# Window attention and a SoLU block on one core: the high and low parts of the probabilities multiplied apart and added in PSUM

## The chip, the core and the metric

One core of one Trainium2 chip runs the whole program. The metric is the device time of one execution in microseconds (us); less is better. Before the change the median of three runs is 497.99 us (497.97 to 498.84). A difference below about 0.2% can't be told from none.

TensorE (PE) multiplies and transposes and writes to PSUM; its weight loads are listed apart as PEld. VectorE is DVE, ScalarE is ACT, GpSimd is POOL, and SP issues the DMA transfers. Each engine works through its own queue in order.

## What is computed

The input has 4 sequences of 768 tokens with 8 heads of 64. Attention sees a window of 128 tokens back and a few sink tokens at the start of the sequence; a SoLU block with a normalisation follows, with 3072 tokens in all.

```python
scores = scale * np.matmul(q, k.transpose(0, 1, 3, 2))
keep = is_sink | in_window            # 4 sinks, window of 128
scores = np.where(keep, scores, -1000000000.0)
a = np.exp(scores - np.max(scores, axis=-1, keepdims=True))
a = a / (np.sum(a, axis=-1, keepdims=True) + 1e-09)
attn = np.matmul(a, v)
x = attn.transpose(0, 2, 1, 3).reshape(B * S, H * D)
h = x @ w_in                          # 512 -> 1024
sm = softmax(h)
solu = h * sm
ln = (solu - mu) / np.sqrt(var + 1e-06) * g_ln
return ln @ w_out                     # 1024 -> 512
```

All of it is float32.

## The kernel before

**Two parts for each number.** PE multiplies operands that are rounded to a shorter format (float32r) at a higher rate than full float32. To keep the accuracy the kernel splits an operand into a high part, the rounded value, and a low part, the remainder, and adds the products of the parts. `w1h` and `w1l`, `w2h` and `w2l` are the two parts of the weights; `xh` and `xl`, `uh` and `ul` those of the tokens.

**Chunks.** The 3072 tokens are worked on in 24 chunks of 128, numbered n. A chunk belongs to sequence b and has place c in it; two sequences alternate. Chunks with c = 0 (n = 0, 1, 12, 13) open a sequence and see neither an earlier chunk nor sinks; the first two of them (`native(n)`) are calculated in full float32. The other 22 chunks are the ones whose value products are touched by the change.

**From scores to tokens.** For each chunk: `score` multiplies queries and keys of one head into the PSUM tile `s` (264 columns, or 128 where c = 0); `mask` and `exps` make exponentials `sc`; `normalise` divides; `turn_p` transposes four heads at a time on PE. A half block hb is four heads. `p_hi` and `p_lo` write the high and the low part of the transposed probabilities into one tile `pt`, [128 keys, 4 heads, 2 parts, 128 queries]. For c > 0 `part_new` makes `pc` (what belongs to this chunk's own keys) and `part_old` leaves in `pt` what belongs to the chunk before in the sequence (n − 2).

**The value products.** The tile `vs` holds for each pair of heads the columns (head 0 high, head 0 low, head 1 low, head 1 high), 64 each. With two of these as weights, one product gives in rows 0 to 63 of PSUM the product with one part of v and in rows 64 to 127 that with the other. `value(n, pr)` works on one pair of heads, four times in a chunk: per head one product with `pc` and one with `pt`, each of 256 columns (both parts of the probabilities side by side), and one of 256 columns for the sinks of both heads, with weights `vsink` and the tile `skt`. They land in a PSUM tile `av`, [128, 2 heads, 2 parts, 128 queries].

**Adding up.** Four things have to be added for each head: two parts of v by two parts of the probabilities. `gather` adds the two parts of the probabilities with a reduction on DVE from PSUM into `y`. `shift` moves the other rows' half of `y` with two DMA transfers into `ysh`, so that both parts of v lie in the same rows, and `tokens` adds them on GpSimd into `xt`, two additions for a half block. Then `x_hi` (ScalarE) and `x_lo` (GpSimd) split `xt` into `xh` and `xl`, and `hidden` multiplies these by the first weights into `h`.

**After that** come the SoLU block with its exponential, centring and transposes (`turn_u`, tile `utp`), `u_hi`, `u_lo`, the second product `project` into `o`, `scale` and `store`.

**Buffers.** PSUM tiles `av`, `o`, `skp` (the transposed sink probabilities) and `xp` share a pool of two buffers (`ps_acc`). SBUF tiles `y`, `ysh` and `xt` have two buffers each.

**The order.** It is written out as numbers. `PLAN` gives each step a time relative to its chunk (16 units apart), `FIRST` shifts the chunks that open a sequence, `OWN` has own numbers for the first four chunks and the last two, and `PLAN_W` places the preparation of the weights. The steps are sorted by these numbers and issued in that order; each engine's queue follows from it.

Of the kernel before, what the change touches and what calls it, by code (L numbers as in the profile page):

```python
# [9 lines left out]
F32 = mybir.dt.float32  # L10
# [9 lines left out]
    "load_k": (-44.81,),  # L20
    "load_q": (-59.03,),
    "load_v": (-41.29,),
    "turn_q": (-42.19,),
    "turn_k": (-38.38,),
    "take_q": (-40.61, -40.67),
    "rest_q": (-38.96, -39.06),
    "swap_q": (-38.11, -38.3),
    "keep_k": (14.29,),
    "take_k": (-36.14, -35.45),
    "rest_k": (-35.7, -35.33),  # L30
    "ring_sinks": (-36.19,),
    "score": (-33.44, -29.74, -32.95, -26.95, -28.22, -30.8, -25.49, -21.19),
    "pick": (-32.47, -28.68, -32.31, -26.85, -27.27, -29.01, -24.23, -20.88),
    "mask": (-32.28, -28.41, -32.14, -26.44, -27.23, -28.94, -24.21, -20.59),
    "exps": (-26.81, -24.4, -23.54, -18.95),
    "invert": (-22.96, -18.09),
    "normalise": (-18.87, -15.91),
    "turn_p": (-17.35, -13.82),
    "p_hi": (-16.64, -11.13),
    "p_lo": (-15.83, -9.87),  # L40
    "part_new": (-12.34, -8.49),
    "part_old": (-10.63, -5.19),
    "sinks_hi": (-16.77, -15.48),
    "sinks_lo": (-15.95, -14.62),
    "v_hi": (-29.55, -32.12),
    "v_lo": (-13.37, -18.76),
    "sink_values": (8.06,),
    "turn_sinks": (-10.59,),
    "take_sinks": (-9.42,),
# [4 lines left out]
    "x_hi": (2.13, 8.46),  # L54
    "x_lo": (7.3, 10.78),
    "hidden": (9.12, 11.84, 11.95, 15.93, 9.13, 11.85, 13.94, 15.92),
    "highest": (18.08, 18.07),
    "peak": (18.67,),
    "solu_exp": (20.25,),
    "solu": (21.78,),  # L60
    "centre": (23.78,),
    "square": (29.22,),
    "variance": (30.73,),
    "root": (37.78,),
    "turn_u": (26.36, 26.47, 33.28, 34.25),
    "u_hi": (28.38, 35.48),
    "u_lo": (29.27, 35.93),
    "project": (32.84, 34.47, 35.03, 36.66, 37.58, 37.8, 39.25, 40.19),
    "scale": (41.34,),
    "store": (56.2,),  # L70
}
PLAN_W = {
    "round_ident": (-3163.34,),
    "gains": (-344.53, -1257.3, -494.63, -210.32, 7.7, -70.04, -35.97, -251.92, -3187.03),
    "outside": (181.94,),
    "fetch_small": (-3957.07, -334.9, -3898.57),
    "scalars": (-1567.28,),
    "spread": (-1567.18, -1257.7),
    "take_small": (-1567.08, -1257.5),
    "masks": (-1279.21, -432.35, -165.0),  # L80
    "fetch_w": (-405.15, -3960.38, -426.29, -3880.5, -3919.36, -3952.13, -3953.56, -417.09, -3892.48, -3917.91,
                -3984.79, -352.47, -151.19, -383.05, -132.13, -412.11),
    "lower_w": (-322.59, -1511.91, -340.85, -464.5, -1518.94, -3256.59, -3271.05, -342.81, -551.25, -1488.73,
                -3298.13, -259.68, -126.59, -247.18, -65.79, -329.82),
    "move_w": (-278.19, -1291.02, -319.05, -426.7, -1268.02, -2053.29, -2135.99, -342.63, -474.7, -1311.88, -2065.14,
               -242.49, -126.04, -206.92, -64.64, -318.86),
    "sign_w": (-159.49, -1266.75, -280.91, -419.12, -514.59, -2051.66, -2009.32, -327.68, -447.58, -1267.77,
               -2054.73, -219.39, -79.66, -139.64, -54.37, -316.39),
    "rest_w": (-155.59, -517.15, -155.98, -388.61, -341.51, -2042.38, -1259.65, -242.66, -366.45, -1238.15, -521.74,
               -206.56, -69.38, -91.58, -32.25, -243.78),  # L90
    "sum_w": (-119.83, -422.04, -96.33, -336.21, -229.53, -1475.65, -702.46, -156.13, -302.03, -648.8, -436.66,
              -80.12, 29.82, -32.53, 15.53, -217.15),
    "w_hi": (-128.31, -479.01, -100.46, -341.71, -328.13, -1468.88, -984.48, -230.1, -337.05, -577.13, -482.82,
             -120.05, -19.66, -38.33, -27.91, -142.74),
    "less_w": (-118.42, -381.66, -88.15, -328.34, -206.16, -1389.51, -691.27, -137.84, -264.23, -448.45, -338.06,
               -54.35, 33.19, -26.02, 16.19, -99.77),
    "w_lo": (-100.5, -348.23, -79.88, -324.36, -159.61, -1257.51, -570.51, -129.19, -260.8, -350.76, -260.82, -44.19,
             33.91, -21.12, 20.58, -87.29),
# [3 lines left out]
    "load_k": -44.94, "load_q": -26.01, "load_v": -1.72, "turn_q": -0.63, "turn_k": -1.52, "take_q": -0.56,  # L102
    "rest_q": 1.16, "swap_q": 1.2, "keep_k": -15.24, "take_k": -2.22, "rest_k": -0.04, "ring_sinks": 19.87,
    "score": -0.52, "pick": -141.4, "mask": 0.1, "exps": -0.49, "invert": 0.8, "normalise": 1.65, "turn_p": 2.88,
    "p_hi": 2.39, "p_lo": 3.57, "part_new": -91.77, "part_old": 14.12, "sinks_hi": -15.13, "sinks_lo": 80.96,
    "v_hi": 6.27, "v_lo": 0.87, "sink_values": -17.46, "turn_sinks": -111.76, "take_sinks": 33.57, "value": -0.23,
    "gather": -0.6, "shift": -0.41, "tokens": 1.81, "x_hi": 0.92, "x_lo": 0.06, "hidden": -0.59, "highest": -1.19,
    "peak": -0.51, "solu_exp": 2.24, "solu": 1.9, "centre": 0.58, "square": -3.38, "variance": -3.55, "root": 0.7,
    "turn_u": 0.05, "u_hi": 1.02, "u_lo": 0.95, "project": 0.45, "scale": 4.92, "store": -8.36,
}  # L110
OWN = {
# [61 lines left out]
P = 128  # L173
# [56 lines left out]
def _banded(ctx, tc, q, k, v, n_sink, window, w_in, w_out, g_ln, out, val, wts, wpool, consts):  # L230
# [467 lines left out]
    def take_sinks(n, _):  # L698
        if place(n)[1] > 0:
            tr = st["skp", n]  # L700
            skt = st["skt", n] = sb.tile([P, 2, P], F32R, tag="skt", name=f"skt_{n}", bufs=2)
            for i, m in enumerate((even, odd)):
                nc.scalar.activation(skt[:, i, :], tr.bitcast(F32), AF.Copy, scale=m)

    def value(n, pr):
        b, c = place(n)
        hb, jp = divmod(pr, HB // 2)
        alone = c == 0
# [333 lines left out]
```

## Time and profile before

| | |
|---|---|
| median of three runs | 497.99 us |
| the profiled execution | 498.57 us |
| its span, first to last instruction | 496.9 us |
| mean granted clock of PE | 0.988 |
| products on PE, as many weight loads | 2631 |
| transfers of `ysh` / of `qX` | 88 / 88 |

A profile page has the busy time of each engine first, then the span in 40 slices of 12.4 us in which a digit is the busy share in tenths. Lines of groups name the source line, the engine, the operation, output and inputs by the program's tile names, the shape and count, then busy us and mean ns of one, and the idle time of the engine just before them with what ended it. A product's length reaches from its start to its modelled end, and products overlap; the distance from one start to the next tells what a product takes of PE. In the view of waits a line says who waited for whom, with total us, times and the longest.

### The profile page before, as it was taken

To read this page: it belongs to the slowest core of one execution; us is meant where nothing else is said; L and a number is where in the kernel's file an instruction comes from. 1 tells how busy PE (TensorE), PEld (TensorE's weight loads), DVE (VectorE), ACT (ScalarE), POOL (GpSimd) and SP (SyncE) were. 2 spreads that over 40 slices of the span, in tenths; PEclk is the share of its full clock that TensorE was granted. 3 is DMA by queue.
4 is the path that set the end of the run, shared out by engine and by line. 5 is a ranking of instruction groups with operands and counts; after the bars stand their busy time and mean duration, and the time that the engine had idled before them with its cause. 6 is when DMAs were issued, how large, how long until landed. Compare 5 with 4: busy or idle time off the path is not lost.

```text
span 496.9 us, 9093 instructions
## 1 busy us (share of the span) xinstructions
PE 468.7 (94%) x2631; PEld 388.4 (78%) x2631; DVE 390.5 (79%) x1195; ACT 354.4 (71%) x957; POOL 316.1 (64%) x439
## 2 busy tenths in 40 slices
PE   0989999999899999999999999999999999999995
PEld 0444767888788888888888888888888888887873
DVE  2878999899987588798799988888888879766631
ACT  4798997787785667776876786676777787675352
POOL 3675576588666557678646386676776776667610
PEclk9978999999999999999999999999999999999999
DMA  8966154354265353522555363464264262201101
GB/s 275 307 196 171 43 108 106 85 122 113 61 140 119 75 117 84 120 67 54 119 136 106 79 139 68 113 138 107 53 141 106 54 144 61 57 28 44 44 22 47
DMA packets 101099, 51.78 MB, mean 104 GB/s; under 512 B 78956, under 2 KB 90228, under 8 KB 101044
## 3 DMA queue, kind: packets, MB, share of 16 engines
q1 hardware_dynamic: 101044, 51.14, 42.4%
q8 instruction: 23, 0.38, 0.3%
q14 instruction: 32, 0.26, 0.2%
HBM read 27.53 MB, written 6.42 MB: 68 GB/s over the span
## 4 chain that ended last, share of the span: by engine, by line
PE 73%; DVE 9%; ACT 5%; POOL 5%; issue 4%; DMA 2%; SPq 0%; DVEq 0%; POOLq 0%
PE o L841 22%; PE h L772 21%; PE s L606 4%; PE s L607 4%; PE utp L826 4%; PE av L721 3%; PE ptp L652 3%; PE av L724 3%; PE ws L441 2%; PE kt L526 2%; PE qt L526 2%; PE av L726 1%; DVE y L734 1%; DVE ring L579 1%; DMA wraw<-in_moe_w_in_dram 1%
## 5 line engine op out<-in xcount | busy, mean ns | idle before, releaser
L841 PE MATMUL o<-w2h,uh 128*128 128x512 f32 x192 | 79.2, 412 | 0.0
L772 PE MATMUL h<-w1h,xh 128*128 128x512 f32 x192 | 77.5, 403 | 0.6 <-DVE u L794 0.6
L634 ACT ACTIVATE sc<-sc,nmx 128x136 f32<-128x136 f32 (+1 forms) x192 | 76.4, 402 | 1.7 <-DVE nmx L624 1.2
L772 PE MATMUL h<-w1l,xh 128*128 128x512 f32 x192 | 75.9, 395 | 0.0
L841 PE MATMUL o<-w2h,ul 128*128 128x512 f32 x192 | 75.7, 394 | 0.0
L734 DVE TENSOR_REDUCE y<-av 128x256 f32<-128x512 f32 x88 | 60.3, 687 | 19.5 <-PE av L726 17.0
L772 PE MATMUL h<-w1h,xl 128*128 128x512 f32 x192 | 75.7, 394 | 0.0
L841 PE MATMUL o<-w2l,uh 128*128 128x512 f32 x192 | 75.6, 394 | 0.0
L669 POOL TENSOR_SCALAR_AFFINE_SELECT pc<-pt 128x1024 fp32r<-128x1024 f32 x40 | 43.8, 1095 | 33.3 <-DVE pt L662 17.0
L624 DVE CUSTOM_DVE_ANT_0 sc<-s,bias 128x136 f32<-128x136 f32 (+1 forms) x192 | 54.4, 295 | 10.1 <-PE s L604 2.9
L645 POOL TENSOR_TENSOR sc<-sc,rs 128x544 f32<-128x544 f32 (+1 forms) x48 | 52.2, 1089 | 15.5 <-DVE rs L640 8.7
L606 PE MATMUL s<-ring,qT 128*128 128x264 f32 (+1 forms) x176 | 56.2, 321 | 2.6 <-DVE nmx L624 1.4
L761 POOL TENSOR_TENSOR xl<-xt,xh 128x256 fp32r<-128x256 f32 x44 | 32.4, 737 | 28.9 <-ACT xh L756 22.5
L607 PE MATMUL s<-ring,qX 128*128 128x264 f32 (+1 forms) x176 | 49.7, 285 | 0.3 <-DMA qX<-qT 0.3
L721 PE MATMUL av<-pc,vs 128*128 128x256 f32 x160 | 44.3, 299 | 1.3 <-ACT ob L846 0.9
L675 POOL TENSOR_SCALAR_AFFINE_SELECT pt<-pt 128x1024 fp32r<-128x1024 f32 x40 | 43.6, 1091 | 1.6
L830 ACT CAST uh<-utp 128x512 fp32r<-128x512 f32 x48 | 28.0, 586 | 21.3 <-PE utp L826 21.1
L834 DVE TENSOR_TENSOR ul<-utp,uh 128x512 fp32r<-128x512 f32 x48 | 33.0, 687 | 12.8 <-ACT uh L830 12.1
L772 PEld LDWEIGHTS h<-w1h,xl 128*128 128x128 f32 x192 | 36.1, 188 | 8.9
L841 PEld LDWEIGHTS o<-w2h,ul 128*128 128x128 f32 x192 | 36.1, 188 | 8.7 <-DVE ul L834 0.2
L606 PEld LDWEIGHTS s<-ring,qT 128*128 128x128 f32 x176 | 33.1, 188 | 11.9 <-issue 3.6
L574 ACT CAST ring<-kt 64x512 fp32r<-64x512 f32 x44 | 25.4, 578 | 22.9 <-DVE ring L579 21.8
(147 smaller groups left out, 1300.7 us busy)
## 6 DMA issues: line engine op xcount, KB each, us to landing
qX<-qT SPq DMA_DIRECT2D x88, 128.0 KB, 2.2
kn<-in_k_dram SPq DMA_DIRECT2D x24, 256.0 KB, 3.5
qn<-in_q_dram SPq DMA_DIRECT2D x24, 256.0 KB, 4.1
vn<-in_v_dram SPq DMA_DIRECT2D x24, 256.0 KB, 4.3
out_dram<-ob SPq DMA_DIRECT2D x24, 256.0 KB, 3.5
ysh<-y SPq DMA_DIRECT2D x88, 64.0 KB, 2.0
wraw<-in_moe_w_out_dram SPq DMA_DIRECT2D x8, 512.0 KB, 4.0
wraw<-in_moe_w_in_dram SPq DMA_DIRECT2D x8, 512.0 KB, 6.6
```

Source lines behind the costliest of these rows:

```text
L606: nc.tensor.matmul(o, st["qT", n, x][:, r, :], rhs, start=True, stop=False)
L607: nc.tensor.matmul(o, st["qX", n, x][:, r, :], rhs, start=False, stop=True)
L624: nc.vector.tensor_tensor_reduce(out=st["sc", n, hb][:, j, c0:c1], in0=st["s", n, h].rearrange("p a x -> p (a x)")[:, c0:c1], in1=bias0 if ...
L634: nc.scalar.activation(sc[:, i, c0:c1], sc[:, i, c0:c1], AF.Exp, bias=nmx[:, i:i + 1], scale=-1.0, accum_out=ssum[:, i:i + 1])
L645: nc.gpsimd.tensor_tensor(sc[:, :, c0:c1], sc[:, :, c0:c1], rs.unsqueeze(2).to_broadcast([P, HB, c1 - c0]), op=ALU.mult)
L669: nc.gpsimd.affine_select(pc, pt.bitcast(F32), pattern=[[0, HB * 2], [1, P]], compare_op=ALU.is_ge, fill=0.0, base=0, channel_multiplier=-1)
L675: nc.gpsimd.affine_select(pt, pt.bitcast(F32), pattern=[[0, HB * 2], [-1, P]], compare_op=ALU.is_ge, fill=0.0, base=-1, channel_multiplier=1)
L721: nc.tensor.matmul(acc[:, x], lhs, pc[:, 2 * jp + x], start=(x == 0), stop=(alone and x == 1))
L734: nc.vector.tensor_reduce(st["y", n, hb][:, jp], st["acc", n, pr].rearrange("p x s q -> p x q s"), axis=AX.X, op=ALU.add)
L772: nc.tensor.matmul(st["h", n][:, cols], a[:, kt % 2, :], w[:, kt, cols], start=(kt == 0 and m == 0), stop=(kt == KT1 - 1 and m == 2))
L834: nc.vector.tensor_tensor(ul, st["utp", n, g4], st["uh", n, g4].bitcast(F32), op=ALU.subtract)
L841: nc.tensor.matmul(st["o", n], a[:, kt % 4, :], part(w, kt), start=(kt == 0 and m == 0), stop=(kt == KT2 - 1 and m == 2))
```

## The change

`value` now works on a half block (two pairs of heads) at a time, so that it stands twice in a chunk, not four times. Each product of 256 columns becomes two of 128, one for the high part of the probabilities (t = 0) and one for the low part (t = 1), with the same weights and into the same 128 columns of PSUM, where they are added up. The tile `av` now holds [128, 2 pairs, 2 heads, 128 queries] and serves the whole half block. The sinks' product stays at 256 columns.

`gather`, `shift` and the tile `y` are gone. A new step `lower` copies the half of `av` that lies in the other rows into `ysh` with ScalarE, and `tokens` adds the other half to it on DVE, straight from PSUM. Both have two instructions of 64 rows by 256 elements for a half block.

All numbers of `PLAN`, `FIRST`, `OWN` and `PLAN_W` are new; one line of them stands here for all.

```diff
 PLAN = {
-    "value": (-5.58, -9.27, -2.3, -0.4),
-    "gather": (-4.96, -7.67, -1.44, 1.33),
-    "shift": (-3.45, 1.72),
-    "tokens": (0.47, 7.55),
+    "value": (-8.65, 1.15),
+    "lower": (-7.68, 3.4),
+    "tokens": (-7.23, 3.74),
...
-    def value(n, pr):
+    def value(n, hb):
...
-        acc = st["acc", n, pr] = ps_acc.tile([P, 2, 2, P], F32, tag="acc", name=f"av_{n}_{pr}")
-        for x in range(2):
-            lhs = st["vs", n, hb][:, jp, 2 * x:2 * x + 2, :].rearrange("p t d -> p (t d)")
-            nc.tensor.matmul(acc[:, x], lhs, pc[:, 2 * jp + x], start=(x == 0), stop=(alone and x == 1))
+            if jp == 0:
+                acc = st["acc", n, hb] = ps_acc.tile([P, HB // 2, 2, P], F32, tag="acc", name=f"av_{n}_{hb}")
+            parts = [(n, pc)] if alone else [(n, pc), (n - 2, pt)]
+            for x in range(2):
+                for m, p_ in parts:
+                    lhs = st["vs", m, hb][:, jp, 2 * x:2 * x + 2, :].rearrange("p t d -> p (t d)")
+                    for t in range(2):
+                        nc.tensor.matmul(acc[:, jp, x, :], lhs, p_[:, 2 * jp + x, t, :],
+                                         start=(x == 0 and m == n and t == 0),
+                                         stop=(alone and x == 1 and t == 1))
             if not alone:
-                lhs = st["vs", n - 2, hb][:, jp, 2 * x:2 * x + 2, :].rearrange("p t d -> p (t d)")
-                nc.tensor.matmul(acc[:, x], lhs, pt[:, 2 * jp + x], start=False, stop=False)
-        if not alone:
-            nc.tensor.matmul(acc[:, :, 0, :], st["vsink", b][:, pr, :], st["skt", n], start=False, stop=True)
+                nc.tensor.matmul(acc[:, jp], st["vsink", b][:, pr, :], st["skt", n], start=False, stop=True)
...
-        nc.vector.tensor_reduce(st["y", n, hb][:, jp], st["acc", n, pr].rearrange("p x s q -> p x q s"),
-                                axis=AX.X, op=ALU.add)
...
-        nc.sync.dma_start(ysh[0:D], y[D:P, :, 0, :])
-        nc.sync.dma_start(ysh[D:P], y[0:D, :, 1, :])
...
-        nc.gpsimd.tensor_tensor(xt[0:D], y[0:D, :, 0, :], ysh[0:D], op=ALU.add)
-        nc.gpsimd.tensor_tensor(xt[D:P], y[D:P, :, 1, :], ysh[D:P], op=ALU.add)
+    def lower(n, hb):
...
+        for x in range(2):
+            nc.scalar.copy(ysh[ROWS[x]], st["acc", n, hb][ROWS[1 - x], :, x, :])
...
+        for x in range(2):
+            nc.vector.tensor_tensor(xt[ROWS[x]], st["acc", n, hb][ROWS[x], :, x, :], st["ysh", n, hb][ROWS[x]], op=ALU.add)
```

In the rows below the names carry chunk, half block or pair, and a running number: `av_11_1` is chunk 11's tile for pair 1 before, and `av_11_0` that for half block 0 afterwards.

PE before, at the second pair of chunk 11:

```order
L606 MATMUL s_12_6_3340<-ring_124,qT_12_0_3089 128x128
L607 MATMUL s_12_6_3340<-ring_124,qX_12_0_3158 128x128
L721 MATMUL av_11_1_3349<-pc_11_0_3289,vs_11_0_3001 128x256
L724 MATMUL av_11_1_3349<-pt_11_0_3215,vs_9_0_2447 128x256
L721 MATMUL av_11_1_3349<-pc_11_0_3289,vs_11_0_3001 128x256
L724 MATMUL av_11_1_3349<-pt_11_0_3215,vs_9_0_2447 128x256
L726 MATMUL av_11_1_3349<-skt_11_3346,vsink_1_927 128x2x128
L841 MATMUL o_8_3244<-w2h_3_521,uh_8_1_3287 128x512
```

PE now, at the same half block of chunk 11, of which the first pair and the start of the second are shown:

```order
L831 MATMUL o_8_3354<-w2h_2_608,ul_8_1_3398 128x512
L722 MATMUL av_11_0_3428<-pc_11_0_3374,vs_11_0_3067 128x128 x2
L722 MATMUL av_11_0_3428<-pt_11_0_3288,vs_9_0_2487 128x128 x2
L722 MATMUL av_11_0_3428<-pc_11_0_3374,vs_11_0_3067 128x128 x2
L722 MATMUL av_11_0_3428<-pt_11_0_3288,vs_9_0_2487 128x128 x2
L726 MATMUL av_11_0_3428<-skt_11_3400,vsink_1_1140 128x256
L722 MATMUL av_11_0_3428<-pc_11_0_3374,vs_11_0_3067 128x128 x2
```

Five products per pair became nine, and both pairs of a half block now stand in one run of eighteen, where before each pair's five stood apart between other work.

PE now, from the end of chunk 10's last value products on. Six more products into `o_8` and then `skp_11` follow; `skp_11` takes the `ps_acc` buffer that `av_10_1` has held:

```order
L726 MATMUL av_10_1_3310<-skt_10_3127,vsink_0_658 128x256
L522 MATMUL qt_13_3333<-ident_89,qn_13_2697 128x128 x4
L602 MATMUL s_12_1_3344<-ring_124,qT_12_1_3142 128x128
L603 MATMUL s_12_1_3344<-ring_124,qX_12_1_3202 128x128
L648 MATMUL ptp_11_1_3349<-ident_89,sc_11_1_3050 128x128 x4
L831 MATMUL o_8_3354<-w2h_0_245,uh_8_0_3241 128x512
L831 MATMUL o_8_3354<-w2l_0_246,uh_8_0_3241 128x512
L831 MATMUL o_8_3354<-w2h_0_245,ul_8_0_3245 128x512
L602 MATMUL s_12_4_3366<-ring_124,qT_12_0_3144 128x128
```

Eight transposes, four scores and nine products of 512 columns stand between the last value product of chunk 10 and the sinks' transpose of chunk 11.

DVE before, around the first half block of chunk 11:

```order
L734 TENSOR_REDUCE y_11_0_3384<-av_11_1_3349 128x256
L639 TENSOR_SCALAR rs_12_0_3400<-ssum_12_0_3225 128x4
L640 RECIPROCAL rs_12_0_3400<-rs_12_0_3400 128x4
L557 TENSOR_TENSOR qT_13_1_3355<-qt_13_3314,qT_13_1_3355 64x512
L557 TENSOR_TENSOR qT_13_0_3357<-qt_13_3314,qT_13_0_3357 64x512
L734 TENSOR_REDUCE y_11_0_3384<-av_11_0_3412 128x256
```

DVE now, at the same place:

```order
L553 TENSOR_TENSOR qT_13_1_3418<-qt_13_3333,qT_13_1_3418 64x512
L553 TENSOR_TENSOR qT_13_0_3420<-qt_13_3333,qT_13_0_3420 64x512
L742 TENSOR_TENSOR xt_11_0_3467<-av_11_0_3428,ysh_11_0_3460 64x256 x2
L635 TENSOR_SCALAR rs_12_0_3475<-ssum_12_0_3292 128x4
L636 RECIPROCAL rs_12_0_3475<-rs_12_0_3475 128x4
```

The two reductions are replaced by two additions in one place, which read `ysh_11_0` that ScalarE's two copies write. On ScalarE these copies stand ahead of the exponentials of chunk 12 and of `xh_11_0`.

More of the change, by code (lines that the diff above doesn't have):

```diff
@@ L64 @@
[L64 to L70, printed above, removed]
+    "load_k": (-42.11,),
+    "load_q": (-56.77,),
+    "load_v": (-40.64,),
+    "turn_q": (-42.08,),
+    "turn_k": (-38.33,),
+    "take_q": (-40.71, -40.74),
+    "rest_q": (-39.71, -39.83),
+    "swap_q": (-36.9, -38.18),
+    "keep_k": (16.66,),
+    "take_k": (-36.03, -35.95),
@@ new lines @@
+    "rest_k": (-35.93, -35.59),
+    "ring_sinks": (-37.22,),
+    "score": (-33.6, -30.15, -33.83, -27.32, -28.37, -31.53, -26.07, -20.81),
+    "pick": (-33.39, -29.96, -33.7, -26.66, -27.87, -30.58, -24.45, -20.23),
+    "mask": (-31.87, -28.4, -32.39, -26.45, -27.72, -30.49, -24.37, -20.22),
+    "exps": (-23.69, -23.17, -19.12, -19.11),
+    "invert": (-22.5, -18.36),
+    "normalise": (-21.74, -16.4),
+    "turn_p": (-17.82, -12.73),
+    "p_hi": (-16.75, -11.19),
+    "p_lo": (-16.32, -8.73),
@@ new lines @@
+    "part_new": (-11.64, -5.81),
+    "part_old": (-11.53, -5.08),
+    "sinks_hi": (-17.18, -15.11),
+    "sinks_lo": (-16.87, -13.95),
+    "v_hi": (-29.9, -31.63),
+    "v_lo": (-12.23, -20.21),
+    "sink_values": (9.27,),
+    "turn_sinks": (-11.15,),
+    "take_sinks": (-9.87,),
+    "value": (-8.65, 1.15),
+    "lower": (-7.68, 3.4),
+    "tokens": (-7.23, 3.74),
+    "x_hi": (-6.19, 4.81),
+    "x_lo": (-5.05, 8.49),
+    "hidden": (10.53, 11.7, 13.21, 14.61, 7.5, 11.71, 13.2, 16.91),
+    "highest": (17.71, 17.72),
@@ L71 @@
+    "peak": (18.98,),
+    "solu_exp": (20.8,),
+    "solu": (22.39,),
+    "centre": (23.96,),
+    "square": (31.56,),
+    "variance": (36.13,),
+    "root": (37.67,),
+    "turn_u": (26.8, 26.46, 30.84, 30.62),
+    "u_hi": (28.16, 33.03),
+    "u_lo": (28.71, 37.94),
+    "project": (35.34, 36.02, 36.56, 37.29, 38.56, 39.34, 39.39, 42.47),
+    "scale": (44.9,),
+    "store": (58.0,),
 }
 PLAN_W = {
-    "round_ident": (-3163.34,),
-    "gains": (-344.53, -1257.3, -494.63, -210.32, 7.7, -70.04, -35.97, -251.92, -3187.03),
@@ L75 @@
[L75 to L84, printed above, removed]
@@ L97 @@
-    "w_lo": (-100.5, -348.23, -79.88, -324.36, -159.61, -1257.51, -570.51, -129.19, -260.8, -350.76, -260.82, -44.19,
-             33.91, -21.12, 20.58, -87.29),
+    "round_ident": (-1322.39,),
+    "gains": (-368.15, -1165.53, -479.33, -225.74, -20.3, -46.93, -60.03, -262.5, -3645.13),
+    "outside": (211.35,),
+    "fetch_small": (-4191.48, -394.17, -4097.18),
+    "scalars": (-1537.76,),
+    "spread": (-1368.02, -1361.85),
+    "take_small": (-1358.56, -1336.69),
+    "masks": (-1097.56, -360.46, -185.65),
@@ new lines @@
+    "sign_w": (-227.21, -621.59, -467.19, -417.3, -573.87, -2082.04, -1376.57, -338.9, -576.28, -1319.96, -2083.31,
+               -210.97, -119.38, -128.9, -79.1, -366.13),
+    "rest_w": (-173.68, -604.59, -319.07, -404.26, -377.17, -1351.58, -1346.0, -317.8, -571.46, -1311.07, -1320.96,
+               -171.48, -109.56, -122.6, -69.94, -359.9),
+    "sum_w": (-128.69, -443.97, -113.39, -361.19, -269.27, -1347.16, -530.33, -174.79, -364.93, -549.25, -475.14,
+              -145.58, -13.22, -36.37, 27.53, -248.08),
@@ new lines @@
+    "w_hi": (-159.19, -519.26, -113.21, -324.89, -327.46, -1325.09, -1307.62, -283.17, -477.5, -509.0, -1268.36,
+             -148.15, -31.62, -94.11, 30.19, -173.9),
+    "less_w": (-125.3, -417.49, -109.98, -313.61, -215.74, -1292.57, -517.46, -174.67, -308.17, -400.9, -453.55,
+               -130.49, -8.51, -31.52, 30.44, -123.76),
+    "w_lo": (-122.59, -378.07, -92.59, -284.69, -189.42, -1264.65, -485.74, -151.02, -283.72, -378.99, -383.81,
+             -129.95, -4.1, -21.98, 32.36, -112.0),
@@ L107 @@
-    "gather": -0.6, "shift": -0.41, "tokens": 1.81, "x_hi": 0.92, "x_lo": 0.06, "hidden": -0.59, "highest": -1.19,
-    "peak": -0.51, "solu_exp": 2.24, "solu": 1.9, "centre": 0.58, "square": -3.38, "variance": -3.55, "root": 0.7,
-    "turn_u": 0.05, "u_hi": 1.02, "u_lo": 0.95, "project": 0.45, "scale": 4.92, "store": -8.36,
+    "load_k": -44.89, "load_q": -25.65, "load_v": 6.01, "turn_q": -4.31, "turn_k": 1.85, "take_q": -0.49,
+    "rest_q": 0.01, "swap_q": 0.6, "keep_k": -15.73, "take_k": -0.34, "rest_k": 0.19, "ring_sinks": 20.63,
@@ new lines @@
+    "score": 0.23, "pick": -141.32, "mask": -0.21, "exps": -0.17, "invert": 0.83, "normalise": 2.08, "turn_p": 1.83,
+    "p_hi": 1.7, "p_lo": 1.86, "part_new": -101.27, "part_old": 13.79, "sinks_hi": -15.91, "sinks_lo": 83.7,
+    "v_hi": -0.04, "v_lo": -0.3, "sink_values": -12.59, "turn_sinks": -108.85, "take_sinks": 34.56, "value": -1.18,
+    "lower": -0.7, "tokens": 0.05, "x_hi": 0.57, "x_lo": 1.43, "hidden": -0.13, "highest": -0.13, "peak": 1.2,
+    "solu_exp": 1.97, "solu": 0.74, "centre": 0.26, "square": 0.73, "variance": -1.65, "root": 2.29, "turn_u": -0.06,
@@ L728, in gather @@
-    def gather(n, pr):
+        pc = pt if alone else st["pc", n, hb]
+        for jp in range(HB // 2):
+            pr = hb * (HB // 2) + jp
+            if native(n):
+                if ("xp", n, hb) not in st:
+                    st["xp", n, hb] = ps_acc.tile([P, HB // 2, P], F32, tag="acc", name=f"xp_{n}_{hb}")
+                for x in range(2):
+                    nc.tensor.matmul(st["xp", n, hb][ROWS[x], jp, :], st["vn", n][:, 2 * pr + x, :],
+                                     pt[:, 2 * jp + x, 0, :], start=True, stop=True)
+                continue
+            if jp == 0:
+                acc = st["acc", n, hb] = ps_acc.tile([P, HB // 2, 2, P], F32, tag="acc", name=f"av_{n}_{hb}")
+            parts = [(n, pc)] if alone else [(n, pc), (n - 2, pt)]
+            for x in range(2):
+                for m, p_ in parts:
[4 more added lines that the diff above has]
+                                         stop=(alone and x == 1 and t == 1))
+            if not alone:
+                nc.tensor.matmul(acc[:, jp], st["vsink", b][:, pr, :], st["skt", n], start=False, stop=True)
@@ L729, in gather @@
+    def lower(n, hb):
         if native(n):
             return
-        hb, jp = divmod(pr, HB // 2)
-        if ("y", n, hb) not in st:
-            st["y", n, hb] = sb.tile([P, HB // 2, 2, P], F32, tag="y", name=f"y_{n}_{hb}", bufs=2)
-        nc.vector.tensor_reduce(st["y", n, hb][:, jp], st["acc", n, pr].rearrange("p x s q -> p x q s"),
-                                axis=AX.X, op=ALU.add)
-    def shift(n, hb):
-        if native(n):
-            return
-        y = st["y", n, hb]
         ysh = st["ysh", n, hb] = sb.tile([P, HB // 2, P], F32, tag="ysh", name=f"ysh_{n}_{hb}", bufs=2)
-        nc.sync.dma_start(ysh[0:D], y[D:P, :, 0, :])
-        nc.sync.dma_start(ysh[D:P], y[0:D, :, 1, :])
+        for x in range(2):
+            nc.scalar.copy(ysh[ROWS[x]], st["acc", n, hb][ROWS[1 - x], :, x, :])
@@ L855, in _banded @@
               score, pick, mask, exps, invert, normalise, turn_p, p_hi, p_lo, part_new, part_old, sinks_hi, sinks_lo,
-              v_hi, v_lo, sink_values, turn_sinks, take_sinks, value, gather, shift, tokens, x_hi, x_lo,
+              v_hi, v_lo, sink_values, turn_sinks, take_sinks, value, lower, tokens, x_hi, x_lo,
               hidden, highest, peak, solu_exp, solu, centre, square, variance, root, turn_u, u_hi, u_lo,
```

73 lines of the change are left out of this document (7 added, 66 removed), and 109 rows, old and new, of the table OWN.

## The prediction

> **What bounds the kernel now.** I read the busy times first, then the slices, then busy time by stretch.
>
> ```profile
> span 496.9 us, 9093 instructions
> PE 468.7 (94%) x2631; PEld 388.4 (78%) x2631; DVE 390.5 (79%) x1195; ACT 354.4 (71%) x957; POOL 316.1 (64%) x439
> PE   0989999999899999999999999999999999999995
> PEclk9978999999999999999999999999999999999999
> ```
>
> PE leads with 94% of the span, and its slices show where the other 6% lie: in the first slices and at the end. The granted clock is full but for the start, so products run at one speed from about 40 us on. The view of busy time by stretch gives the share in the middle (columns: length, then each engine's busy us and count, clock, DMA):
>
> ```profile
> 0.00:80.00 80.00, 62.21 (x283) 40.42 (x284) 61.61 (x182) 64.34 (x167) 45.08 (x81) 0.94 0.64 177
> 80.00:460.00 380.00, 375.77 (x2200) 323.14 (x2199) 314.91 (x984) 275.71 (x766) 261.00 (x346) 1.00 0.41 95
> 460.00:497.00 37.00, 30.70 (x152) 24.80 (x151) 14.00 (x30) 14.40 (x25) 10.02 (x14) 0.97 0.12 38
> ```
>
> From 80 to 460 us PE is busy 375.8 of 380 us. It is the bound there, with 4.2 us idle, while DVE has 65 us to spare, ScalarE 104 and GpSimd 119. All `av` products but a few lie in that stretch. Whatever PE gets to do there in addition lengthens the kernel by nearly its full size; whatever DVE, GpSimd or the DMA queue are spared can return 4.2 us at most there. The view of waits says what PE waited for:
>
> ```profile
> PE spread L302 <- POOL alone L296: 7.3, 1, 7.3
> PE ws L441 <- DVE wbits L424: 4.7, 1, 4.7
> PE av L721 <- ACT ob L846: 0.9, 2, 0.7
> ```
>
> The two long waits belong to the scalars and the weights at the start, which the change does not touch (only their places in the order shift). The rest are below 2 us each in sum. No wait of PE names `gather`, `shift` or `tokens` as its releaser for more than fractions of a microsecond.
>
> **What the change puts on PE.** The groups of instructions give the counts (line, names, shape, count, busy us, mean ns):
>
> ```profile
> L721 PE MATMUL av<-pc,vs 128*128 128x256 f32 x160 | 44.3, 299 | 1.3 <-ACT ob L846 0.9 <-DVE y L734 0.3
> L724 PE MATMUL av<-pt,vs 128*128 128x256 f32 x160 | 41.5, 281 | 0.0
> L721 PE MATMUL av<-pt,vs 128*128 128x256 f32 x16 | 3.5, 300 | 0.0
> ```
>
> That is 336 products of 256 columns. Each becomes two of 128 columns that add into the same 128 columns of PSUM: 672 in place of 336. The 80 sink products keep their 256 columns. The mean of about 0.28 us is one product's length from its start to its modelled end; products overlap, so the price is the distance between starts. The timeline of PE shows it for one pair of heads (start, length):
>
> ```profile
> 184.60 0.28 PE L721 MATMUL av<-pc,vs 128*128 128x256 f32 x1
> ...
> 185.07 0.28 PE L726 MATMUL av<-skt,vsink 128*128 128x256 f32 x1
> 185.19 0.40 PE L841 MATMUL o<-w2h,uh 128*128 128x512 f32 x1
> ```
>
> From 184.60 to 185.19 us stand five products (the three left out are the other two of L721 and L724 and start between): 0.59 / 5 = **0.118 us** for one of 256 columns.
>
> A product of 128 columns in the same number format stands in this trace too: the scores of the chunks that open a sequence. Four of them lie between products of 512 columns:
>
> ```profile
> 253.24 0.40 PE L841 MATMUL o<-w2h,ul 128*128 128x512 f32 x1
> 253.47 0.22 PE L606 MATMUL s<-ring,qT 128*128 128x128 f32 x1
> 253.53 0.27 PE L607 MATMUL s<-ring,qX 128*128 128x128 f32 x1
> 253.65 0.28 PE L606 MATMUL s<-ring,qT 128*128 128x128 f32 x1
> 253.76 0.27 PE L607 MATMUL s<-ring,qX 128*128 128x128 f32 x1
> 253.87 0.45 PE L841 MATMUL o<-w2h,uh 128*128 128x512 f32 x1
> 254.16 0.39 PE L841 MATMUL o<-w2l,uh 128*128 128x512 f32 x1
> ```
>
> A product of 512 columns takes 0.23 us (253.24 to 253.47). From 253.47 to 254.16 are 0.69 us for four of 128 columns and one of 512: (0.69 − 0.23) / 4 = **0.115 us** each. Half the columns cost almost the same. Why, the weight loads of the same stretch tell:
>
> ```profile
> 253.48 0.19 PEld L607 LDWEIGHTS s<-ring,qX 128*128 128x128 f32 x1
> 253.59 0.19 PEld L606 LDWEIGHTS s<-ring,qT 128*128 128x128 f32 x1
> 253.70 0.19 PEld L607 LDWEIGHTS s<-ring,qX 128*128 128x128 f32 x1
> 253.81 0.19 PEld L841 LDWEIGHTS o<-w2h,uh 128*128 128x128 f32 x1
> ```
>
> Loads follow each other at 0.11 us and no closer. A product of 256 columns just covers the next load; one of 128 doesn't, and the load sets the pace. The change reads the two 128-column parts against the same weights, so the question is whether the second load is made. Before has the same case, `uh` against `w2h` and then against `w2l`:
>
> ```profile
> L841 PEld LDWEIGHTS o<-w2l,uh 128*128 128x128 f32 x192 | 36.3, 189 | 4.2 <-issue 0.2
> L841 PEld LDWEIGHTS o<-w2h,uh 128*128 128x128 f32 x192 | 36.2, 189 | 4.5 <-PE ptp L652 0.2
> ```
>
> Each of the two has its own 192 loads: equal weights are loaded again.
>
> So PE gets 672 × 0.112 − 336 × 0.118 = 75.3 − 39.6 = **+35.6 us**, with 0.112 between the load's 0.110 and the measured 0.115. By the ends: 672 × 0.110 gives +34.3, 672 × 0.115 gives +37.6.
>
> The Trainium skill speaks against this rate in one place: TensorE: Matmul & The Clock Gate, section Back-to-back issue gap, has about 81 ns per product of 128 columns for a stream of load and product. By that the 672 would take 54.4 us and the change +14.8 us. The rows above, 0.110 to 0.115 us, don't agree; what they leave of it is the second rival.
>
> **What it takes from the others and puts on them.**
>
> ```profile
> L734 DVE TENSOR_REDUCE y<-av 128x256 f32<-128x512 f32 x88 | 60.3, 687 | 19.5 <-PE av L726 17.0 <-issue 2.0 <-POOL pc L669 0.4
> L751 POOL TENSOR_TENSOR xt<-y,ysh 64x256 f32<-64x256 f32 x44 | 32.1, 730 | 10.0 <-DMA ysh<-y 6.8 <-DVE z L802 3.1
> L752 POOL TENSOR_TENSOR xt<-y,ysh 64x256 f32<-64x256 f32 x44 | 32.3, 734 | 3.3
> ysh<-y SPq DMA_DIRECT2D x88, 64.0 KB, 2.0
> L756 ACT CAST xh<-xp 128x256 fp32r<-128x256 f32 x4 | 1.5, 364 | 0.0
> L761 DVE TENSOR_TENSOR xl<-xp,xh 128x256 fp32r<-128x256 f32 x4 | 1.7, 417 | 0.0
> ```
>
> Gone: 88 reductions (60.3 us of DVE), 88 additions on GpSimd (32.1 + 32.3 = 64.4 us), 88 transfers of `ysh` on SP's queue at 2.0 us to landing. New: 88 copies from PSUM on ScalarE and 88 additions from PSUM on DVE, each of 256 elements in 64 rows. The nearest rows with 256 elements from PSUM take 364 and 417 ns, so 32.0 and 36.7 us. These operations aren't in the trace with 64 rows; the ends I take are half these prices and the 687 ns of the reduction, at most 60.5 us on either engine. ScalarE comes to 354.4 + 32.0 = 386.4 us (415 at the upper end), DVE to 390.5 − 60.3 + 36.7 = 366.9 us (at most 390.7), GpSimd to 316.1 − 64.4 = 251.7 us. None nears PE's 468.7 + 35.6 = 504.3 us, so all of this is hidden behind PE, in both directions, and I cost it at nothing. If the cover went, ScalarE's part would be the first to show.
>
> The path from an `av` tile to `x_lo` gets shorter: two transfers and two additions of 0.73 us go, two copies and two additions, 2 × 0.364 + 2 × 0.417 = 1.56 us, come. That can return part of the 4.2 us that PE idles in the middle. Ends: nothing and 4.2; I take 3.
>
> **Sum.** The profiled execution took 498.57 us (0.6 above the median 497.99 of three, inside their spread to 498.84). 498.6 + 35.6 − 3 = 531.2, so **531 us**. This case's own range: from the median, 498.0 + 34.3 − 4.2 = 528, less 4 for a start that may come out better in the new order, 524; above, 498.6 + 37.6 with nothing returned and 6 us of new waits, 542.
>
> **Rivals.**
>
> First, the other side: **the second product pays no load.** If equal weights were kept, or their load fully hidden, a product of 128 columns would cost 0.059 us, half of 0.118; PE would get nothing, 672 × 0.059 = 39.6 for 39.6, and the shorter path would return 3 us: 498.6 − 3 = 495.6, faster. It decides below (39.6 + 3) / 672 = 0.063 us per product. For it: the recorded starts 253.47 and 253.53 lie 0.06 apart. Against: the next starts lie 0.12 and 0.11 apart, the 512-column product after the four takes 0.29 in place of 0.23, and the doubled loads of `uh`. 4 in 100. That the change doesn't do what it says, in that a repeated load is dropped, comes to the same.
>
> Second, **every other load is half hidden.** If all pairs went like the first (253.47 to 253.65, 0.18 us for two), PE would get 336 × (0.18 − 0.118) = +20.8: 498.6 + 20.8 − 3 = 516 us. Against: the first pair follows a long product, under which its loads began; in a run of 16 only the first does. 10 in 100.
>
> Third, **a new wait for PSUM.** The sinks' transpose `skp` takes the buffer that the last `av` tile of the chunk before held, which now is free only after copies and additions, 1.56 us and the waits in two queues; both queues run in order, so a late copy holds up the exponentials behind it, and the addition behind it on DVE holds up the masks. In front of `skp` stand nine products of 512 columns alone, 9 × 0.23 = 2.1 us, and more. If it came 1 us late in each of the 20 chunks with sinks, 498.6 + 35.6 + 20 = 554 us. 9 in 100.
>
> **Chances.** 77 in 100 for 524 to 542 us, 10 for the second rival, 9 for the third, 4 for the first. The range 513 to 544 holds the likeliest case and the second rival, 0.87 by these numbers; the third is left out above and the first below, and the half-hidden load keeps the low end. A difference under 0.2% (1 us) can't be told from none here. Faster 0.03, same 0.01, slower 0.96: the first rival alone can end faster or near no change.
>
> **What would show it.** PEld with 2631 + 336 = 2967 loads and `av` starts 0.11 us apart through a run of eight: right. Starts 0.06 apart: the first rival. PE 98 to 100% busy in the middle, with a total near 504 us, and DVE about 367, ScalarE 386, GpSimd 252: right. A wait of `skp` or `av` for the copies or additions above 10 us in all: the third rival. The prediction fails if a product of 128 columns costs well under 0.11 us in a long run, or if PE waits more in the new order than in the old.

## The result and the profile after

The changed kernel takes 525.14 us (median of four runs, 524.73 to 529.21), the kernel before 498.06 us beside it: a ratio of 1.055, with an interval of 1.052 to 1.058. It is slower by 27 us. The forecast was 531 us, in a range from 513 to 544.

The page after, first lines:

```profile
span 523.7 us, 9609 instructions
PE 500.8 (96%) x2967; PEld 420.6 (80%) x2967; DVE 370.1 (71%) x1195; ACT 390.1 (74%) x1045; POOL 255.0 (49%) x351
PE   1989999999999999999999999999999999999994
```

PE is busy for 32.1 us longer (500.8 against 468.7) with 336 more products and 336 more loads, and it idles for 22.9 us of the span where it idled for 28.2. PE's sum stays 3.5 us under the 504.3 of the prediction; the account below comes back to that. DVE, ScalarE and GpSimd come within 4 us of theirs. Busy time by stretch, after (columns as in the prediction):

```profile
0.00:80.00 80.00, 66.21 (x318) 43.80 (x319) 62.20 (x184) 67.36 (x176) 46.81 (x83) 0.98 0.68 187
80.00:460.00 380.00, 378.55 (x2350) 330.51 (x2349) 282.96 (x939) 291.65 (x801) 189.83 (x246) 1.00 0.32 78
460.00:487.00 27.00, 27.00 (x161) 23.22 (x161) 14.26 (x48) 16.88 (x45) 13.49 (x16) 1.00 0.05 20
487.00:524.00 37.00, 29.06 (x143) 23.11 (x141) 10.67 (x27) 14.18 (x24) 4.87 (x7) 0.97 0.07 24
```

In the middle PE now idles for 1.5 of 380 us (4.2 before), in the first 80 us for 13.8 (17.8 before), and the granted clock of that stretch is 0.98 instead of 0.94. DVE has 97 us to spare in the middle, GpSimd 190. The longest waits of PE, after:

```profile
PE spread L298 <- POOL alone L292: 9.1, 1, 9.1
PE ws L437 <- DVE wbits L420: 1.1, 1, 1.1
PE o L831 <- ACT ob L836: 0.8, 2, 0.5
```

No wait of `skp` or `av` for the new copies and additions (`ysh`, `xt`) is in that view, which goes down to 0.2 us. The products themselves, the timeline of PE after, at one half block (x2: two products in a row with one line and one pair of tiles):

```profile
206.96 0.33 PE L722 MATMUL av<-pc,vs 128*128 128x128 f32 x2
207.13 0.39 PE L722 MATMUL av<-pt,vs 128*128 128x128 f32 x2
207.35 0.39 PE L722 MATMUL av<-pc,vs 128*128 128x128 f32 x2
207.58 0.38 PE L722 MATMUL av<-pt,vs 128*128 128x128 f32 x2
207.80 0.34 PE L726 MATMUL av<-skt,vsink 128*128 128x256 f32 x1
207.98 0.33 PE L722 MATMUL av<-pc,vs 128*128 128x128 f32 x2
...
208.81 0.34 PE L726 MATMUL av<-skt,vsink 128*128 128x256 f32 x1
208.99 0.40 PE L831 MATMUL o<-w2h,uh 128*128 128x512 f32 x1
```

Behind the first pair, pairs of products stand 0.22 us apart, 0.11 each. The eighteen products of the half block take 208.99 − 206.96 = 2.03 us; the ten of before took 2 × 0.59 = 1.18. The loads of the same half block:

```profile
207.07 0.30 PEld L722 LDWEIGHTS av<-pt,vs 128*128 128x128 f32 x2
207.30 0.30 PEld L722 LDWEIGHTS av<-pc,vs 128*128 128x128 f32 x2
207.52 0.30 PEld L722 LDWEIGHTS av<-pt,vs 128*128 128x128 f32 x2
207.74 0.19 PEld L726 LDWEIGHTS av<-skt,vsink 128*128 128x128 f32 x1
```

Each pair shows two loads of the same weights, and pairs of loads too are 0.22 us apart. What replaced the reductions and the transfers:

```profile
L734 ACT COPY ysh<-av 64x256 f32<-64x256 f32 x88 | 32.3, 367 | 17.4 <-PE av L726 16.4
L742 DVE TENSOR_TENSOR xt<-av,ysh 64x256 f32<-64x256 f32 x88 | 37.1, 421 | 21.6 <-ACT ysh L734 19.6
```

367 and 421 ns, where 364 and 417 were taken. DVE waits for the copies 19.6 us in sum, and none of it shows as a wait of PE.

### The profile page after: what moved, and what is told of

Its sections match the earlier page's. It is cut to its first block, busy times and chain, and to the rows that moved or that the text cites. A ratio compares the mean times of both kernels' runs of the same rounds, so it can differ in the third digit from the quotient of the medians.

```text
span 523.7 us, 9609 instructions
## 1 busy us (share of the span) xinstructions
PE 500.8 (96%) x2967; PEld 420.6 (80%) x2967; DVE 370.1 (71%) x1195; ACT 390.1 (74%) x1045; POOL 255.0 (49%) x351
## 4 chain that ended last, share of the span: by engine, by line
PE 84%; DVE 2%; ACT 1%; issue 1%; DMA 1%; DVEq 0%; ACTq 0%
PE h L762 25%; PE o L831 23%; PE av L722 14%; PE s L602 4%; PE utp L816 4%; PE s L603 4%; PE ptp L648 3%; PE av L726 3%; PE qt L522 2%; PE kt L522 2%; DMA wraw<-in_moe_w_out_dram 1%; ACT ob L836 1%; PE ws L437 0%; DVE u L784 0%; DMA qX<-qT 0%
## 5 line engine op out<-in xcount | busy, mean ns | idle before, releaser
L831 PE MATMUL o<-w2h,uh 128*128 128x512 f32 x192 | 80.7, 420 | 1.0 <-ACT ob L836 0.8
L722 PE MATMUL av<-pt,vs 128*128 128x128 f32 x352 | 66.1, 275 | 0.0
L620 DVE CUSTOM_DVE_ANT_0 sc<-s,bias 128x136 f32<-128x136 f32 (+1 forms) x192 | 55.6, 294 | 12.9 <-PE s L603 6.7
L722 PE MATMUL av<-pc,vs 128*128 128x128 f32 x320 | 58.3, 264 | 0.0
L722 PEld LDWEIGHTS av<-pc,vs 128*128 128x128 f32 x320 | 51.1, 190 | 3.4 <-issue 0.5
L722 PEld LDWEIGHTS av<-pt,vs 128*128 128x128 f32 x352 | 52.4, 192 | 0.0
L742 DVE TENSOR_TENSOR xt<-av,ysh 64x256 f32<-64x256 f32 x88 | 37.1, 421 | 21.6 <-ACT ysh L734 19.6
L609 DVE COPY_PREDICATED s<-m_cur,s 128x128 f32<-128x128 int32 x96 | 27.5, 291 | 32.6 <-PE s L603 31.8
L734 ACT COPY ysh<-av 64x256 f32<-64x256 f32 x88 | 32.3, 367 | 17.4 <-PE av L726 16.4
```

What stands on the lines that cost most here:

```text
L620: nc.vector.tensor_tensor_reduce(out=st["sc", n, hb][:, j, c0:c1], in0=st["s", n, h].rearrange("p a x -> p (a x)")[:, c0:c1], in1=bias0 if ...
L722: nc.tensor.matmul(acc[:, jp, x, :], lhs, p_[:, 2 * jp + x, t, :], start=(x == 0 and m == n and t == 0), stop=(alone and x == 1 and t == 1))
L734: nc.scalar.copy(ysh[ROWS[x]], st["acc", n, hb][ROWS[1 - x], :, x, :])
L742: nc.vector.tensor_tensor(xt[ROWS[x]], st["acc", n, hb][ROWS[x], :, x, :], st["ysh", n, hb][ROWS[x]], op=ALU.add)
L831: nc.tensor.matmul(st["o", n], a[:, kt % 4, :], part(w, kt), start=(kt == 0 and m == 0), stop=(kt == KT2 - 1 and m == 2))
```

## The experiments

Two questions are open in the result. Is the price of the products really the 35.6 us of the prediction, when only 27 us came out? And what returned the rest? Each run's median stands beside that of the kernel before on the same chip; comparisons with the changed kernel go by its 525.14 us, which was measured apart from these runs.

### The split alone, in the old order

The kernel before, with the value products alone split; they write the same columns as before, and `gather`, `shift`, `tokens` and the order stay.

```diff
-            nc.tensor.matmul(acc[:, x], lhs, pc[:, 2 * jp + x], start=(x == 0), stop=(alone and x == 1))
+            for t in range(2):
+                nc.tensor.matmul(acc[:, x, t, :], lhs, pc[:, 2 * jp + x, t, :], start=(x == 0 and t == 0),
+                                 stop=(alone and x == 1 and t == 1))
...
```

The product with `pt` is split in the same way.

> The kernel before with nothing changed but the value products: each of 256 columns becomes two of 128, which write the same columns of av as before; gather, shift, tokens and the order stay. If a product of 128 columns costs a weight load, 0.112 us (theory), PE gets the full 35.6 us and the old order returns at most the 4.2 us of its idle time in the middle: 529 to 534 us. If the 27 us of the change are the price of the products alone (rival: 0.099 us per product, nothing returned elsewhere): 525 us. If the second product of equal weights pays no load: 498 us.

Measured: 529.61 us against 498.69, a ratio of 1.062 (1.060 to 1.065), 31 us more. Its first 80 us and its middle stretch:

```profile
0.00:80.00 80.00, 62.26 (x300) 41.10 (x301) 61.62 (x182) 64.47 (x168) 47.41 (x83) 0.98 0.66 180
80.00:460.00 380.00, 378.32 (x2349) 331.62 (x2347) 303.50 (x932) 259.33 (x722) 242.60 (x320) 1.00 0.41 92
```

That is the theory's case, and the split by itself costs more than the whole change. PE idles for 1.7 us of the middle, where it idled for 4.2: the old order returns its idle time there too, with the old path. So shorter transfers were not needed for that; PE having more to do was enough.

### The new order and path without the split

The changed kernel with value products of 256 columns.

```diff
-                    for t in range(2):
-                        nc.tensor.matmul(acc[:, jp, x, :], lhs, p_[:, 2 * jp + x, t, :],
...
+                    nc.tensor.matmul(acc[:, jp], lhs, p_[:, 2 * jp + x],
...
```

> The changed kernel with its order and its copies and additions, but the value products back at 256 columns, 336 of them, written over both heads' columns of av, so that the parts of the probabilities are not added up but mixed between heads. If the products cost 35.6 us and new order and path return some 8 us (theory): 525.1 - 35.6 = 489 to 491 us, under the kernel before. If the products cost 27 us and nothing is returned (rival): 498 us.

Measured: 492.31 us against 498.69, a ratio of 0.989 (0.984 to 0.995), with runs from 489.9 to 495.8. The median lies 1 us above the theory's range, far from the rival's 498. It is 6 us under the kernel before, and 33 us under the changed kernel; the sums are mixed between heads, so this is a measurement and no replacement. With the run above this makes a table of four, and the split costs 31 us in the one order and 33 in the other:

| | products of 256 | products of 128 |
|---|---|---|
| old order and path | 498.7 | 529.6 |
| new order and path | 492.3 | 525.1 |

### Fewer columns, as many products

The changed kernel, the low part's products with 32 columns.

```diff
                     for t in range(2):
-                        nc.tensor.matmul(acc[:, jp, x, :], lhs, p_[:, 2 * jp + x, t, :],
+                        w = P if t == 0 else 32
+                        nc.tensor.matmul(acc[:, jp, x, 0:w], lhs, p_[:, 2 * jp + x, t, 0:w],
```

> The changed kernel with the low part's products of 32 columns in place of 128: three quarters of the low part of the probabilities are left out, the number of products stays. If the load sets the pace (theory), no change: 524 to 526 us. If the columns did (rival), 336 x 0.04 = 13 us less: 512 us.

Measured: 523.79 us (522.88 to 524.25), 1.3 us below the changed kernel. Of the 13 us that the columns would have given, nothing is to be seen beyond that. PE's timeline at a half block:

```profile
206.20 0.29 PE L723 MATMUL av<-pc,vs 128*128 128x128 f32 x2
206.34 0.37 PE L723 MATMUL av<-pt,vs 128*128 128x128 f32 x2
206.56 0.38 PE L723 MATMUL av<-pc,vs 128*128 128x128 f32 x2
...
208.02 0.36 PE L727 MATMUL av<-skt,vsink 128*128 128x256 f32 x1
208.22 0.40 PE L832 MATMUL o<-w2h,uh 128*128 128x512 f32 x1
```

Here x2 stands for one product of 128 and one of 32 columns. The half block takes 208.22 − 206.20 = 2.02 us, against 2.03 with full columns. The columns don't set the pace; what stays the same is one load of 128 columns for each product.

### Half the products

The changed kernel without the low part's products.

```diff
-                    for t in range(2):
+                    for t in range(1):
...
```

> The changed kernel without the low part's products: 336 products of 128 columns in place of 672. Theory: 336 x 0.112 = 37.6 us less, 487 to 489 us, hardly below 336 products of 256 columns. Rival (0.099 us per product): 492 us. If the second product of equal weights pays no load, 336 x 0.06 = 20 us less: 505 us.

Measured: 488.66 us against 498.69, a ratio of 0.981 (0.979 to 0.983): 36.5 us below the changed kernel, 0.109 us for each of the 336 products taken out. It leaves out the low part of the probabilities and is no replacement. It is only 3.6 us under the run with 336 products of 256 columns: the second 128 columns of such a product are nearly free.

### Where the rest was returned: the order at the start

Four runs put the new numbers under the old steps. The first takes the preparation of the weights and chunks 0 to 3 from the new order, with products of 256 columns and `gather`, `shift` and `tokens`.

```diff
 PLAN_W = {
-    "round_ident": (-3163.34,),
+    "round_ident": (-1322.39,),
...
-    "scalars": (-1567.28,),
+    "scalars": (-1537.76,),
```

> The kernel before with its own steps and 256-column products; only the order of the weights' preparation and of the first four chunks follows the changed kernel's numbers (its value steps split into two pairs, with gather, shift and tokens spaced out behind them). If the part that was returned at the start comes from the order there (theory): 4 to 7 us less than before, 491 to 494 us. If it comes from the shorter path through copies and additions, or from fewer DMA transfers (rival): 498 us, or more where the two orders join badly.

Measured: 510.88 us against 498.43, a ratio of 1.026 (1.023 to 1.029): slower by 12 us. The theory's total (491 to 494) is missed, and what came is the rival's open end, "or more where the two orders join badly", so the total can't tell where the start's gain comes from. The first product into `h` shows the start apart from it; the timelines of PE before, after and in this run:

```profile
54.92 0.47 PE L772 MATMUL h<-w1h,xh 128*128 128x512 f32 x1
```

```profile
50.52 0.39 PE L762 MATMUL h<-w1h,xh 128*128 128x512 f32 x1
```

```profile
49.75 0.39 PE L704 MATMUL h<-w1h,xh 128*128 128x512 f32 x1
```

The lead of 4 to 5 us is there with the old steps, 20 us before the first value product (70 us): it can't come from the new path. A part of it is the clock's: the split in the old order, whose clock at the start was that of the changed kernel (0.98 in the first 80 us), has this product at 53.0 us. The lead is lost later, first in the stretch where the two orders meet:

```profile
80.00:130.00 50.00, 43.83 (x252) 35.76 (x251) 42.37 (x131) 32.83 (x98) 33.95 (x44) 1.00 0.40 87
```

PE idles for 6.2 of 50 us there (0.9 before), and for 9.0 us between 130 and 460 us, where it was 3.4 before.

The second puts all of the new order under the old steps.

> The kernel before with its own steps and 256-column products, and all of its order after the changed kernel's numbers, the value steps split as in the other run. Theory: the order at the start returns 4 to 7 us, the middle is bound by PE as before: 489 to 494 us. Rival (the path returned it, the order does nothing): 498 us. If reductions and transfers don't fit the other order, new waits: above 500 us.

Measured: 543.35 us against 498.43, a ratio of 1.090 (1.087 to 1.093): the third case of the expectation, new waits. The largest of them is that of the scores for the moved queries:

```profile
PE s L539 <- DMA qX<-qT: 15.3, 17, 2.4
```

Their transfers share SP's queue with those of `ysh`, and these hold the queue up more than before while they wait for the reductions:

```profile
SPq L674 <- DVE y L666: 205.9, 37, 14.9
```

The same wait was 117.8 us before. PE idles for 58.3 us of this span, 30 us more than before; the rest of the 45 us isn't accounted for.

Two more runs were to join the start better, with the new numbers for the weights and chunks 0 and 1 alone, and for chunks 0 to 3 but for the steps from `value` to the split of x.

> The kernel before with its own steps and 256-column products; the order of the weights' preparation and of the first two chunks alone follows the changed kernel's numbers, chunks 2 and 3 keep their old places. If the start is returned by the order (theory) and the old order of chunks 2 and 3 joins it well: first hidden product at 49 to 51 us instead of 53 to 55, and 493 to 496 us in all, faster than before. If the order of the start returns nothing that lasts (rival): 498 us or more, because PE waits later by as much.

> As the run with two chunks, but chunks 2 and 3 too follow the changed kernel's numbers up to the value products and from the hidden products on; value, gather, shift, tokens and the split of x keep their old places where the inputs are there in time. Theory: as above, 493 to 496 us. Rival: 498 us or more.

Measured: 506.04 us against 498.76, ratio 1.016 (1.012 to 1.019), and 512.09 us against the same, ratio 1.028 (1.024 to 1.032). Their first products into `h` start at 51.7 and 49.5 us, and neither keeps the lead: both totals are the rival's. A better start under the old order gave no faster kernel here.

### The new path in the old order

The changed kernel's steps with the old numbers: `value` at the place of the second pair, copies and additions right behind.

```diff
-    "value": (-8.65, 1.15),
-    "lower": (-7.68, 3.4),
-    "tokens": (-7.23, 3.74),
+    "value": (-5.58, -0.4),
+    "lower": (-5.08, 0.1),
+    "tokens": (-4.78, 0.4),
```

> The changed kernel's steps (products of 128 columns, copies on ScalarE, additions on DVE) in the old order: value at the place of the second pair, copies and additions right behind it, all else where the kernel before has it. If the shorter path returns only idle time of the middle and the new order returns the rest at the start (theory): as the split products in the old order, 527 to 530 us. If the path returned all of it (rival): 524 to 526 us, as the changed kernel.

> The same old order and new steps with value products of 256 columns over both heads' columns (the parts of the probabilities are mixed between heads, not added up): the path alone against the kernel before. Theory: the idle time of the middle at most, 494 to 498 us. Rival (the path returned all): 490 to 492 us. If the copies and additions wait badly in the old order: above 500 us.

Measured: 556.36 us against 498.29 with products of 128 columns, ratio 1.117 (1.113 to 1.121), and 526.80 us with products of 256, ratio 1.057 (1.053 to 1.061). Both cases for the first missed, and the second fell into its third, copies and additions that wait badly: the path in this order costs 27 to 29 us, whichever products (556.4 − 529.6, 526.8 − 498.3). What PE waits for most in the run with 256 columns:

```profile
PE s L537 <- DVE ring L510: 10.1, 22, 2.4
PE spread L233 <- POOL alone L227: 7.0, 1, 7.0
PE s L537 <- DVE nmx L555: 5.6, 11, 2.0
```

The keys (`ring`) and the masks' maxima (`nmx`) come from DVE, whose additions stand in the same queue and wait for the copies, 22.4 us in sum. That the additions hold up the keys and masks is argued from the order of the queue, not shown apart; these two waits of PE sum to 15.7 us, and PE idles 18 us longer than before. The split again costs 30 us (556.4 − 526.8). The first products into `h` start at 54.5 us in both, as in the old order.

## Why the prediction was right, point by point

**The bound.** PE is the bound in the middle, and added PE work lengthened the kernel by nearly its size: shown by the split alone (+31 us) and by its removal (−33 us).

**The price of the products, +35.6 us.** Right. Forty half blocks with sinks went from 1.18 to 2.03 us, 40 × 0.85 = 34.0. The four half blocks of chunks 12 and 13 go from four products to eight and from about 4 × 0.118 to 8 × 0.11 us, 4 × 0.41 = 1.6. Together 35.6. Summed over all 44 half blocks of the timelines, from the first start to the next product behind, the value products take 50.5 us in the new order with 256 columns and 85.3 us with 128, 34.8 more. The profiled executions of these two kernels, with mean clocks of 0.997 and 0.995, differ by 35.0 us of span (488.7 and 523.7) and by 35.8 of PE's busy time (465.0 and 500.8); against the kernel before, at a clock of 0.988, the busy time had grown by 32.1. It isn't the columns: with 32 instead of 128 the time stayed, and the loads of equal weights stand in the trace twice. No run tells a load that takes 0.11 us from another fixed cost of 0.11 us for each load with its product, since all of them have loads of 128 columns. The Trainium skill, TensorE: Matmul & The Clock Gate, section LDWEIGHTS, gives a load's time in ns as the columns of the weights over 1.2, an estimate of 107 ns for 128; the 0.11 us between loads agree. The 81 ns per product that the Trainium skill states in the section Back-to-back issue gap of that page for a stream of load and product did not hold, against 0.11 us here; by them the split would have cost an estimated 14.8 us.

**DVE, ScalarE, GpSimd and the transfers at nothing.** Right as to the result: their sums fitted within 4 us, and no wait in the view of PE's waits ended with one of the new copies or additions. But the cover is a matter of the order: the same path in the old order cost 27 to 29 us. The prediction's reason, that the other engines' sums lie far below PE's, would not have told these two apart. That the new order places the copies and additions where nothing behind them is urgent fits both runs, and isn't shown apart.

**What is returned, −3 us.** This term was mis-sized. The profiled executions differ by 26.8 us of span, so 35.6 − 26.8 = 8.8 us were returned. By stretch: idle time of the middle 4.2 − 1.5 = 2.7 us, as forecast; idle time of the first 80 us 17.8 − 13.8 = 4.0 us; a higher granted clock in these 80 us, at most (0.98 − 0.94) × 80 = 3.2 us; and 1.6 us more idle at the end (6.3 in the last 37 us before, 7.9 now). 2.7 + 4.0 + 3.2 − 1.6 = 8.3, near the 8.8. The clock's 3.2 is an upper end: the kernel before took 496.3 to 497.7 us in four runs with mean clocks of 0.994 to 0.998, and 497.0 to 499.9 in those of 0.986 to 0.992, which speaks for 1 to 2 us, an estimate. With the 0.8 us by which the price was taken too high (34.8), 1 to 2 us stay without a place. The 525.14 us lie just inside the low end of the prediction's likeliest band, 524, for which it had taken the full 4.2 us and 4 us for the start. The failed step is the sentence that the change does not touch the waits at the start: the new numbers reorder the weights' preparation. Of its two long waits, `ws` for `wbits` went from 4.7 to 1.1 us and `spread` for `alone` from 7.3 to 9.1. The new order reaches the first `h` 2 to 5 us sooner in every run that has the new numbers for chunks 0 to 3 (49.4 to 50.9 us, against 53.0 to 54.9 in the old order). The first 40 us of the kernel before, of the split in the old order and of the changed kernel show that this isn't the clock alone:

```profile
0.00:40.00 40.00, 24.05 (x78) 13.65 (x79) 25.40 (x67) 27.73 (x62) 21.61 (x43) 0.88 0.82 245
0.00:40.00 40.00, 24.06 (x82) 13.32 (x83) 26.72 (x68) 29.17 (x64) 22.41 (x43) 0.96 0.85 248
0.00:40.00 40.00, 27.40 (x95) 14.35 (x95) 27.89 (x69) 29.80 (x66) 23.03 (x45) 0.96 0.86 263
```

At the same clock of 0.96 PE is busy for 3.3 us more in the new order, with 95 products in place of 82. The run with the old steps under the new start has 96 products by then, so the order gives this, not the path. Only the runs that have the whole new order and the new path kept it in the total; in the others later waits took it back. The start had been given 4 us, but as an end of the range and not in the sum. The clock's part isn't the change's: the split in the old order had 0.98 too.

**The rivals.** No load for equal weights, and half-hidden loads: refuted by the starts 0.11 us apart and by the run without the low part, which saved 0.109 us for each product taken out. A new wait for PSUM: not seen.

**Open.** The new order and the new path together are worth 4 to 6 us (the rows of the table). How much of that is either one's could not be told: the runs that join an order with the other path lost 7 to 45 us. No version with the whole computation that beats the kernel before was found.

## What to carry to other kernels

Where PE is the bound, count its products by the larger of columns and weight load: splitting a product that just covers the next load nearly doubles its price (0.118 to 2 × 0.11 us here), even where the weights stay the same. Work taken off engines that aren't the bound returns the bound's idle time at most; here that was 3 us in the middle, and the split in the old order used up nearly as much without taking anything off. A hand-made order belongs to its steps; an edit and its order have to be judged together, and an estimate must ask what the new order does to parts that the edit doesn't touch.

## What was not expected of the hardware

After a run of loads at 0.11 us, the sinks' product of 256 columns shows 0.18 us to the next start (207.80 to 207.98, 208.81 to 208.99), where such products follow each other at 0.118: the recorded start seems to come before its weights are all in, and the rest is paid then. Single gaps mislead here, and whole runs have to be timed.

The mean granted clock differs between executions of one kernel and can show in the time: the changed kernel's runs with means of 0.993 to 0.997 took 524.7 to 525.4 us, the one with 0.984 took 529.2.
